# Pooled attention and eight experts on one core: from the fourth expert on, x is gathered as quarter rows and turned on VectorE

## The chip, the cores and the metric

The kernel runs on one core of a Trainium2 chip. The metric is the device time of one execution in microseconds (us). A kernel is timed in several executions; the times below are the median and the spread of three. A profile is one execution, recorded by the hardware profiler, and its span is a little shorter than that execution's time, because the start and the end of the program lie outside it.

The core has five engines, each with an instruction stream that it works through in order: TensorE (PE: matmuls and transposes by matmul; its weight loads are listed as PEld), VectorE (DVE), ScalarE (ACT), GpSimd (POOL) and SyncE (SP, which here only issues DMAs). Engines wait for one another through semaphores. An instruction that waits holds up everything behind it on its own engine.

## The reference

First comes attention with pooled keys and values, then a routing that gives each of 4608 tokens to one of eight experts, 576 tokens to each, and then the experts' two matrix products:

```python
def _moe_ref(x, w_gate, w1, w2):
    N, D = x.shape                      # 4608, 512
    E = w_gate.shape[1]; cap = N // E   # 8, 576
    logits = x @ w_gate
    order = np.argsort(-logits.flatten())
    for idx in order:                   # greedy, in order of the logits
        tok, e = idx // E, idx % E
        if assigned[tok] >= 0 or counts[e] >= cap: continue
        assigned[tok] = e; counts[e] += 1
    for e in range(E):
        mask = assigned == e
        h = np.maximum(x[mask] @ w1[e], 0.0)   # w1: 512 x 1024
        out[mask] = h @ w2[e]                  # w2: 1024 x 512
```

Before it, `x` is softmax(q k_p) v_p over 8 batches and 8 heads of 576 positions, with k and v averaged over groups of eight; the rows of `x` are 512 numbers.

## The kernel before

The first 150 us or so are attention. Its result, the rows of `x`, is written to a buffer `xd` in DRAM, 2 KB a row. After that the kernel works expert by expert, numbered e0 to e7 here in the order in which they are worked off. For each expert:

- **Routing** (class `Routing`). An expert's tokens are found by a threshold search (`search`; some rounds, each of nine matmuls of 128x32 on TensorE, small VectorE steps and two small matmuls, the last of them with `ones`), and `close` turns the marked tokens into a list: `eid` is the number of the expert that was closed, `rows` the 576 row numbers as 128 x 5 numbers, `halves` numbers for half rows. `close` ends in eight matmuls with `spread` (L798) that bring the numbers to their partitions, and in two VectorE steps (L802, L806). Routing of one expert runs beside the matrix products of the expert ahead of it, in pieces.
- **x.** `gather` (L1037) fetches 576 rows from `xd` into `xg` by five indirect DMAs on GpSimd, four of 128 rows and one of 64. `xt` turns one of the five tiles of tokens (a "turn"; tiles 0 to 4): four TensorE transposes into the PSUM tile `tp` (L1069), a ScalarE copy to `xh` that rounds to the fast fp32 format (L1071), and a VectorE subtraction that leaves the rest, `xl` (L1073).
- **Weights.** `load_1` and `load_2` fetch w1 and w2 on SP's queue; ScalarE and VectorE split them likewise into high and low parts (`w1h`, `w1l` at L1049, `w2h`, `w2l` at L1058), eight pieces of 128x512 for each matrix.
- **Stage 1** (`stage1`, L1093). Three products, xh·w1h, xh·w1l and xl·w1h, each in four slices of 128, for eight blocks of 128 rows of h: 96 matmuls for columns 0 to 255 (tiles 0 and 1), then 96 for columns 256 to 575 (tiles 2, 3 and 4). So tiles 0 and 1 must be turned when the expert begins, and the other three when the first half of stage 1 ends. The steps after a block are `hh` on ScalarE (L1098) and `hl` on VectorE (L1101).
- **Stage 2** (`stage2`, L1127, and L1132 for the last 64 tokens). 96 matmuls of 512 columns for four tiles of tokens, 16 pairs for the last; then `put` copies the result (`yt`, `yh`) and GpSimd scatters it to `out` by an indirect DMA (`scatter`, L1107).

What stands where in each engine's stream is decided when the program is built, by a planner in `experts`. It has a clock, `now`, that goes forward with every matmul that it emits, and a clock for VectorE, `dve`. Between two matmuls, `advance` may emit what is due: a routing piece (`step`), a piece of a weight split (`Pieces`), a subtraction that was put off (`later`, `flush`), or a turn (`turns`, `turn`). The clock only chooses the order; on the chip each engine goes as fast as its waits allow. One rule for the turns reads

```python
        t = turned.get(e, 5)
        if t < upto and due(e, "rows", 6.5 + 1.3 * t) and now >= last + 1.4 and (fresh or through or t < late):
            last = now
            turn(e, t)
```

so that a turn often stands right behind a routing matmul (`fresh`), and `gather` is emitted in one piece at the routing step that yields `rows`.

Of the kernel before, what the change touches and what calls it, by code (L numbers as in the profile page):

```python
# [423 lines left out]
class Routing:  # L424
# [56 lines left out]
    def more(self):  # L481
# [10 lines left out]
        nc.vector.tensor_scalar(self.spread[:, 96:128], t, 0.0, None, op0=OP.is_equal)  # L492

        self.blk = cst.tile([128, 20, NC], BF, name="blk")
        nc.scalar.activation(self.blk[:, :18], self.i36[:, 1:19, None].to_broadcast([128, 18, NC]), AF.Copy)
# [219 lines left out]
    def close(self, k, last):  # L715
# [58 lines left out]
        for b0, b1 in halves:  # L774
# [19 lines left out]
            t0, t1 = b0 // 4, b1 // 4  # L794
            ps = self.psum()
            for g in range(4):
                for v in range(2):
                    nc.tensor.matmul(ps[:, :t1 - t0], self.spread[:, 96 - 32 * g:224 - 32 * g], cpv[:, v, :, g],  # L798
                                     start=(g == v == 0), stop=(g == 3 and v == 1))
# [184 lines left out]
class Experts:  # L984
# [27 lines left out]

    def load_1(self, eid, q0=0, q1=4):
# [45 lines left out]

    def xt(self, t, name="tp", bufs=2, later=lambda after, t, f: f()):  # L1060

# [5 lines left out]
        ps = self.psA.tile([128, 4, 128], F32, name=name, bufs=bufs)  # L1067
        for j in range(4):
            nc.tensor.transpose(ps[:, j, :n], self.xg[:n, t, 128 * j:128 * j + 128], self.ident[:n, :n])  # L1069
        o = slice(128 * t, 128 * t + n)  # L1070
        nc.scalar.activation(self.xh[:, :, o], ps[:, :, :n], AF.Copy)  # L1071
        xl, xh = self.xl[:, :, o], self.xh[:, :, o].bitcast(F32)
        later(1.3, 0.65, lambda: nc.vector.tensor_tensor(xl, ps[:, :, :n], xh, op=OP.subtract))  # L1073

# [37 lines left out]

    def stage2(self, e, rows, halves, parts=range(5), bank=("h", 5)):
        for t in parts:
            ps = self.psA.tile([128, 512], F32, name=bank[0], bufs=bank[1])
            yield from self.products(e, t, ps)
            self.put(t, ps, rows, halves)
            yield 0.2275 if t < 4 else 0.44
# [17 lines left out]

    def put(self, t, ps, rows, halves):

        if t < 4:
            y = self.wk.tile([128, 512], F32, name="yt", bufs=2)  # L1140
            self.nc.scalar.activation(y, ps, AF.Copy)  # L1141
            self.scatter(self.out, rows[:, t:t + 1], y)
        else:
            y = self.wk.tile([128, 256], F32, name="yh", bufs=2)
            self.nc.scalar.activation(y, ps[:, :256], AF.Copy)
            self.scatter(self.out.rearrange("n (a d) -> (n a) d", a=2), halves, y)

# [54 lines left out]
def experts(ctx, tc, g, R, xd, w1, w2, out, ident, cap, keep):  # L1202
# [15 lines left out]
    now, dve, ready = 0.0, 0.0, 0.0  # L1218

    def later(after, t, f):  # L1220

        waiting.append((now + after, t, f))
# [8 lines left out]
    def step(e):  # L1231

        nonlocal now, ready, dve, fresh, coming, through
        if held:
# [6 lines left out]
        if what == "id":  # L1241

            if p > e or p and pieces[p - 1].l < 8:
                held.append((p, crit, t, what))
                return False
            X.load_1(R.eid, 0, 4 if p else 2)
            eids[p] = R.eid
        elif what == "rows":
            if p and turned[p - 1] < 5:
                held.append((p, crit, t, what))  # L1250
                return False
            X.gather(R.rows, *R.found)
            if R.found[1] == 5:
# [9 lines left out]
    def advance(e, t, quiet=False):  # L1263

        nonlocal now, fresh
        now += t
        fresh = False
        while True:
            if waiting and waiting[0][0] <= now:
                flush(len(waiting) - 1)  # L1270
            elif ready > now or quiet or first(e) or not step(e):
                break

    def due(e, what, t):
# [45 lines left out]
    def turn(e, t, name="tp", bufs=2):  # L1320

        nonlocal now
# [32 lines left out]
    for i in range(4):  # L1355
        w1.next(i < 3)
    since[0, "rows"] = -7.0

    step(0)
# [9 lines left out]
    for e in range(8):  # L1369
# [5 lines left out]
        for n, dt in enumerate(X.stage1(later, not e)):  # L1375
# [5 lines left out]
            if n == (84 if e else 40):  # L1381
                for t in range(turned[e], 5):
                    turn(e, t)
            if n >= 64 and n % 2:
                w2.by((n - 70) // 14 if n > 70 else 0)
# [13 lines left out]
        w1 = pieces[e + 1] = Pieces(e + 1, X.high1, X.low1)  # L1399
        for n, dt in enumerate(X.stage2(e, *toks[e], range(5 if more else 1))):  # L1400

# [5 lines left out]
        if more:  # L1407
# [5 lines left out]
            for t in range(turned[e + 1], 2):  # L1413
                turn(e + 1, t)
        flush(2)
    flush()
    ps = psB.tile([128, 512], F32, name="h", bufs=5)
# [85 lines left out]
```

## Time and profile before

| | |
|---|---|
| median of three executions | 612.34 us (612.32 to 613.32) |
| the profiled execution | 612.35 us |
| its span | 609.9 us |
| mean granted TensorE clock | 0.984 |
| e0 to e7 | from 157.1 us of the span to its end |

The profiled execution's time is the median's to 0.01 us, and 2.45 us of it lie outside the span. In the lines shown below, a group gives the source line, the engine, the operation, what it writes and reads, the count, and busy time or durations; a row of a timeline gives start and duration in us, where "x4" is four like instructions in a row and the duration is that of the group. Matmuls are pipelined, so that four matmuls that start 0.12 us apart overlap in such a row; what one costs in the stream is the distance from start to start.

### The profile page before, as it was taken

How to read it: one execution, taken by the hardware profiler on the slowest of the kernel's cores; microseconds unless marked ns; L12 is line 12 of the kernel's file. 1: busy time of each engine (PE TensorE's matmuls, PEld its weight loads, DVE VectorE, ACT ScalarE, POOL GpSimd, SP SyncE). 2: the span in 40 equal slices, each digit the busy share in tenths (PEclk: the TensorE clock that was granted, in tenths of full speed). 3: DMA queues.
4: the chain of work that ended last, by engine and by line, in shares of the span. 5: the costliest groups of instructions: out<-in, count | busy, mean ns of one | idle time of the engine just before them, and what ended most of it. 6: DMA issues, size and time to landing. Idle time of an engine off the chain costs nothing.

```text
span 609.9 us, 11520 instructions
## 1 busy us (share of the span) xinstructions
PE 591.5 (97%) x4340; PEld 518.3 (85%) x4340; DVE 396.1 (65%) x1164; ACT 240.0 (39%) x562; POOL 177.3 (29%) x222
## 2 busy tenths in 40 slices
PE   8999999985999999999999999999999999999996
PEld 5999999983797799779977987898799889888975
DVE  7578888987885778767964976487367328503500
ACT  7444444461461434233432452255135325513411
POOL 2999999001200500420312301130221123011012
PEclk9999999995999999999999999999999999999999
DMA  8999972223531740616403701540081037014011
GB/s 353 419 420 423 397 274 82 77 100 98 167 116 31 254 147 22 213 62 219 134 35 116 284 1 52 207 174 18 36 323 57 34 120 278 2 52 166 1 40 43
DMA packets 32641, 92.23 MB, mean 151 GB/s; under 512 B 3488, under 2 KB 3488, under 8 KB 29888
## 3 DMA queue, kind: packets, MB, share of 16 engines
q1 hardware_dynamic: 21296, 62.92, 27.5%
q0 software_dynamic: 5952, 19.01, 9.2%
q10 hardware_dynamic: 5328, 9.48, 4.1%
q8 instruction: 35, 0.57, 0.4%
q14 instruction: 30, 0.25, 0.1%
HBM read 72.53 MB, written 18.87 MB: 150 GB/s over the span
## 4 chain that ended last, share of the span: by engine, by line
PE 81%; issue 7%; DVE 4%; DMA 3%; POOL 3%; ACT 1%; SPq 0%; POOLq 0%; ACTq 0%; another core or an unknown queue 0%; DVEq 0%
PE h L1093 32%; PE h L1127 25%; PE psa L272 6%; PE pss L227 5%; PE h L1132 4%; PE tp L1069 3%; DMA rawk<-in_k_dram 2%; PE pse L256 2%; PE rt L256 1%; PE rt L668 1%; DMA out_dram<-yt,rows 1%; PE rt L630 1%; DMA xg<-xd,rows 1%; PE rt L217 1%; DVE e L238 1%
## 5 line engine op out<-in xcount | busy, mean ns | idle before, releaser
L1127 PE MATMUL h<-w2l,hh 128*128 128x512 f32 x256 | 101.8, 398 | 0.0
L1127 PE MATMUL h<-w2h,hh 128*128 128x512 f32 x256 | 101.4, 396 | 0.3 <-PEq L1193 0.3
L1127 PE MATMUL h<-w2h,hl 128*128 128x512 f32 x256 | 101.5, 396 | 0.0
L1107 POOL DMA_INDIRECT out_dram<-yt,rows x29 | 30.3, 1045 | 232.3 <-ACT yt L1141 231.9
L1098 ACT ACTIVATE hh<-h 128x320 fp32r<-128x320 f32 (+1 forms) x128 | 52.5, 410 | 106.6 <-PE h L1093 103.3
L1093 PE MATMUL h<-xh,w1h 128*128 128x320 f32 (+1 forms) x512 | 93.2, 301 | 0.2 <-ACT xh L1071 0.2
L1093 PE MATMUL h<-xl,w1h 128*128 128x320 f32 (+1 forms) x512 | 93.4, 300 | 0.0
L1101 DVE SCALAR_TENSOR_TENSOR hl<-h,hh 128x320 fp32r<-128x320 f32 (+1 forms) x128 | 57.2, 451 | 53.1 <-ACT hh L1098 34.6
L1093 PE MATMUL h<-xh,w1l 128*128 128x320 f32 (+1 forms) x512 | 91.0, 298 | 0.0
L1093 PEld LDWEIGHTS h<-xh,w1h 128*128 128x128 f32 x512 | 75.7, 190 | 3.4 <-issue 2.7
L1093 PEld LDWEIGHTS h<-xl,w1h 128*128 128x128 f32 x512 | 76.1, 190 | 0.4
L1093 PEld LDWEIGHTS h<-xh,w1l 128*128 128x128 f32 x512 | 75.8, 189 | 0.0
L1037 POOL DMA_INDIRECT xg<-xd,rows x40 | 39.3, 982 | 101.9 <-DVE halves L806 52.7
L1141 ACT ACTIVATE yt<-h 128x512 f32<-128x512 f32 x32 | 19.1, 598 | 112.1 <-PE h L1127 67.4
L272 PE MATMUL psa<-vblk,eT 128*128 128x146 f32 (+3 forms) x390 | 59.9, 302 | 0.2
L1127 PEld LDWEIGHTS h<-w2h,hh 128*128 128x128 f32 x256 | 48.2, 188 | 9.3 <-issue 0.7
L1127 PEld LDWEIGHTS h<-w2l,hh 128*128 128x128 f32 x256 | 48.3, 189 | 8.8
L1127 PEld LDWEIGHTS h<-w2h,hl 128*128 128x128 f32 x256 | 48.2, 188 | 8.8
L272 PEld LDWEIGHTS psa<-vblk,eT 128*128 128x128 f32 (+1 forms) x390 | 50.9, 180 | 1.8 <-issue 0.3
L1049 DVE TENSOR_TENSOR w1l<-raw,w1h 128x512 fp32r<-128x512 f32 x64 | 41.7, 685 | 13.4 <-ACT w1h L1045 13.1
L1073 DVE TENSOR_TENSOR xl<-tp,xh 128x512 fp32r<-128x512 f32 (+1 forms) x40 | 25.3, 633 | 37.4 <-ACT xh L1071 37.3
L1058 DVE TENSOR_TENSOR w2l<-raw,w2h 128x512 fp32r<-128x512 f32 x64 | 43.2, 682 | 2.0 <-ACT w2h L1055 1.8
(224 smaller groups left out, 903.3 us busy)
## 6 DMA issues: line engine op xcount, KB each, us to landing
raw<-in_moe_w_dram SPq DMA_DIRECT2D x64, 512.0 KB, 6.3
xd<-xt ACTq DMA_DIRECT2D x36, 256.0 KB, 5.6
rawv<-in_v_dram SPq DMA_DIRECT2D x7, 1280.0 KB, 14.1
rawk<-in_k_dram SPq DMA_DIRECT2D x7, 1152.0 KB, 11.7
rawq<-in_q_dram SPq DMA_DIRECT2D x7, 1152.0 KB, 11.8
rawk<-in_k_dram SPq DMA_DIRECT2D x2, 576.0 KB, 4.7
rawv<-in_v_dram SPq DMA_DIRECT2D x1, 768.0 KB, 8.0
rawq<-in_q_dram SPq DMA_DIRECT2D x1, 640.0 KB, 9.0
```

The source lines that it names most:

```text
L227: nc.tensor.matmul(ps[cols, j // 2, 144 * (j % 2):144 * (j % 2) + 144], self.q_of(b, j, n, cols.stop - cols.start), self.kblk[b % 4][:, j] ...
L272: self.nc.tensor.matmul(o[h], self.eT[i][:, c, h], self.vblk[b % 4][:, self.BLOCKS[c]:self.BLOCKS[c + 1]], start=(c == cs[0]), stop=(c == ...
L1037: nc.gpsimd.indirect_dma_start(out=self.xg[:n, t, :], out_offset=None, in_=self.xd, in_offset=bass.IndirectOffsetOnAxis(ap=rows[:n, t:t + ...
L1049: self.nc.vector.tensor_tensor(l, raw, h.bitcast(F32), op=OP.subtract)
L1058: self.nc.vector.tensor_tensor(self.w2l[:, i], self.raw2[e][:, i], self.w2h[:, i].bitcast(F32), op=OP.subtract)
L1073: later(1.3, 0.65, lambda: nc.vector.tensor_tensor(xl, ps[:, :, :n], xh, op=OP.subtract))
L1093: nc.tensor.matmul(ps[:, :m], a[:, j, fs], b[:, j, o], start=(n == 0), stop=(n == 11))
L1098: nc.scalar.activation(hh[:, f, o], ps[:, :m], AF.Relu)
L1101: later(0.65, 0.4, lambda f=f, o=o, m=m, ps=ps: nc.vector.scalar_tensor_tensor(hl[:, f, o], ps[:, :m], 0.0, hh[:, f, o].bitcast(F32), op0= ...
L1107: st = nc.gpsimd.indirect_dma_start(out=rows, out_offset=bass.IndirectOffsetOnAxis(ap=idx, axis=0), in_=y, in_offset=None)
L1127: nc.tensor.matmul(ps, a[:, f, o], b[:, f], start=(f == 0 and k == 0), stop=(f == 7 and k == 2))
L1132: nc.tensor.matmul(ps[64 * a:64 * a + 64, :256], self.hr[:, f], self.raw2[e][:, f, 256 * a:256 * a + 256], start=(f == 0), stop=(f == 7))
```

## The change

For the experts e3 to e7:

- `close` multiplies the numbers of the list with a constant `copies` (two matmuls of 128x18 more) and VectorE makes `quarters` from it (one step more): 18 x 128 numbers, one for each quarter row of 128 numbers (512 bytes) of the 576 rows, so that the four quarters of a row come to four different groups of 32 partitions.
- `quarter` replaces `gather`: 18 indirect DMAs of 128 quarter rows for each expert instead of five of rows. They are emitted one at a time (`wanted`, `fetch`), on a clock of GpSimd, `pace`, that counts 1.3 for each indirect DMA, and scatters are put off by 1.0 on the planner's clock and take their place in the same order (`stores`).
- `xt` has VectorE transpose the tile in blocks of 32x32, from `xg` into the PSUM tile `tp` (one instruction of 128 x 512 numbers, or 128 x 256 for tile 4, read with a stride of four numbers), instead of the four TensorE transposes. The ScalarE copy and the subtraction stay.
- The slices of x then hold rows 4p+j of x's transposed form in place of rows 128j+p, and `load_1` fetches w1 in the same arrangement.
- The planner counts 1.1 on VectorE's clock for such a turn instead of 0.45 on TensorE's, waits for `landed` (the time of the DMAs by its own count), and lets a turn of e3 to e7 go where VectorE's clock is not ahead. For all experts the conditions of the turns and of `flush` change.

```diff
+        self.copies = cst.tile([128, 4, 32], F16, name="copies")
...
             ps = self.psum()
+            if k > 2:
+                for v in range(2):
+                    nc.tensor.matmul(ps[:, 16:34], self.copies.rearrange("p a i -> p (a i)"), cp[:, v, :18],
+                                     start=(v == 0), stop=(v == 1))
+                self.quarters = wk.tile([128, 18], I32, name="quarters", bufs=3)
+                nc.vector.tensor_scalar(self.quarters, ps[:, 16:34], self.acol, 0.0, op0=OP.add, op1=OP.max)
...
-        src = self.w1[ds(r, 1)].rearrange("o (j p) f -> p (o j) f", p=128)
+        src = self.w1[ds(r, 1)].rearrange("o (p j) f -> p (o j) f" if quarters else "o (j p) f -> p (o j) f", p=128)
...
+    def quarter(self, idx, n):
+        if not n:
+            self.xg = self.buf("xg", [128, 5, 512])
+        t, g = divmod(n, 4)
+        self.nc.gpsimd.indirect_dma_start(out=self.xg[:, t, 128 * g:128 * g + 128], out_offset=None,
+                                          in_=self.xd.rearrange("n (a d) -> (n a) d", a=4),
+                                          in_offset=bass.IndirectOffsetOnAxis(ap=idx[:, n:n + 1], axis=0))
...
-        for j in range(4):
+        if quarters:
+            nc.vector.transpose(ps[:, :, :n].rearrange("p j (g i) -> p g j i", i=32),
+                                self.xg[:, t, :4 * n].rearrange("p (g i j) -> p g j i", j=4, i=32))
+        for j in range(0 if quarters else 4):
             nc.tensor.transpose(ps[:, j, :n], self.xg[:n, t, 128 * j:128 * j + 128], self.ident[:n, :n])
...
-        later(1.3, 0.65, lambda: nc.vector.tensor_tensor(xl, ps[:, :, :n], xh, op=OP.subtract))
+        later(1.8 if quarters else 1.3, 0.65, lambda: nc.vector.tensor_tensor(xl, ps[:, :, :n], xh, op=OP.subtract))
...
+    def quarters(e):
+        return e > 2
+    def fetch():
+        nonlocal pace
+        e, n, idx = wanted.pop(0)
+        X.quarter(idx, n)
+        pace = max(pace, now) + 1.3
+        if n % 4 == 3 or n == 17:
+            landed[e, n // 4] = pace + 3.7
...
+        if stores and now >= stores[0][0]:
+            stores.pop(0)[1]()
+            pace = max(pace, now) + 1.3
+        elif wanted and now >= pace:
+            fetch()
...
-        now = max(now, since[e, "rows"] + 6.0 + 1.3 * t) + 0.45
+        while (e, t) not in landed:
+            fetch()
+        now = max(now, landed[e, t])
         flush(1)
-        X.xt(t, name, bufs, later_low)
+        if quarters(e):
+            dve = max(dve, now) + 1.1
+        else:
+            now += 0.45
+        X.xt(t, name, bufs, later_low, quarters(e))
...
-        if t < upto and due(e, "rows", 6.5 + 1.3 * t) and now >= last + 1.4 and (fresh or through or t < late):
+        if t < (5 if quarters(e) else upto) and now >= landed.get((e, t), now + 1) + (1.5 if quarters(e) else 0.5) and now >= last + 1.4 and (
+                t < late or (dve <= now if quarters(e) else fresh or through)):
```

The planner's new counts move the routing steps, the turns and the gathers in the streams. The line numbers of the changed kernel differ: matmuls of stage 1 L1093 become L1118, those of stage 2 L1127 become L1152, the turn's L1069 becomes L1091 (VectorE) or L1094 (TensorE, e0 to e2), `xl` L1098, the gathers L1059 and L1049, the scatters L1132. Three places follow.

On TensorE, in the first half of e3's stage 1 (256 columns). Before, the routing of the next expert has closed, its two small matmuls (with `untri` and `tri`) stand there, and the turn of tile 3 stands right behind them:

```order
L1093 MATMUL h<-xh,w1l 128x256 x4
L1093 MATMUL h<-xl,w1h 128x256 x3
L738 LDWEIGHTS untri
L738 MATMUL rt<-ones,untri 128x1
L739 LDWEIGHTS tri
L739 MATMUL rt<-inc,tri 128x1
L1069 MATMUL tp<-ident,xg 128x128 x4
L1093 MATMUL h<-xl,w1h 128x256
```

Now the last small matmul of the search's last round (`ones`, 128x16) stands near the end of that half, 14 matmuls ahead of the first one of the second half (320 columns):

```order
L701 LDWEIGHTS ones
L701 MATMUL rt<-g_254,ones 128x16
L1118 MATMUL h<-xl,w1h 128x256 x2
L1118 MATMUL h<-xh,w1h 128x256 x4
L1118 MATMUL h<-xh,w1l 128x256 x4
L1118 MATMUL h<-xl,w1h 128x256 x4
L1118 MATMUL h<-xh,w1h 128x320 x3
```

The search's end has moved from e2's stage 2 to the end of the first half of e3's stage 1, and no turn stands on TensorE.

On VectorE, at the same end of the search. Before, the steps from `inc` to `eid` are followed by two pieces of w1 and the list's first steps (`si`, `sab`); the turns of tiles 0 to 2 stand ahead of these rows, and those of 3 and 4 behind them:

```order
L729 SCALAR_TENSOR_TENSOR inc<-ones,own 128x36
L731 TENSOR_SCALAR eid<-fm 1x1
L732 TENSOR_SCALAR eid<-eid 1x1
L1049 TENSOR_TENSOR w1l<-raw_3860,w1h 128x512 x2
L1101 SCALAR_TENSOR_TENSOR hl<-h,hh 128x256
L742 SCALAR_TENSOR_TENSOR si<-inc,rt,own 128x36
```

Now the transposes of tiles 3 and 4 stand behind `eid`, with tile 3's subtraction between them:

```order
L736 SCALAR_TENSOR_TENSOR inc<-ones,own 128x36
L738 TENSOR_SCALAR eid<-fm 1x1
L739 TENSOR_SCALAR eid<-eid 1x1
L1091 STREAM_TRANSPOSE tp<-xg 128x4x4x32
L1098 TENSOR_TENSOR xl<-tp,xh 128x4x128
L1091 STREAM_TRANSPOSE tp<-xg 128x2x4x32
L1126 SCALAR_TENSOR_TENSOR hl<-h,hh 128x256
L1080 TENSOR_TENSOR w2l<-raw_4400,w2h 128x512
L1098 TENSOR_TENSOR xl<-tp,xh 128x4x64
L749 SCALAR_TENSOR_TENSOR si<-inc,rt,own 128x36
```

The two last turns of e3 have come behind the search's end on VectorE.

On GpSimd, at e3's list. Before, its five gathers stand between the last scatter of e1 (`yh`) and the first of e2 (`yt`):

```order
L1107 DMA out_dram<-yh,halves 9216x256
L1037 DMA xg<-xd,rows 128x512 x4
L1037 DMA xg<-xd,rows 64x512
L1106 MEMSET spacer 1x1
L1107 DMA out_dram<-yt,rows 4608x512
```

Now twelve of e3's quarter gathers stand among e2's scatters. The last of the twelve is here, behind e2's fourth scatter; the other six of e3 follow e2's last scatter, and then e4's first five, which another list (`quarters_4800`) feeds (the numbers tell the buffers apart):

```order
L1132 DMA out_0_dram<-yt_4357,rows_3392 4608x512
L1049 DMA xg_4165<-xd_62,quarters_4125 128x128
L1131 MEMSET spacer_1808 1x1
L1132 DMA out_0_dram<-yh_4387,halves_3456 9216x256
L1049 DMA xg_4165<-xd_62,quarters_4125 128x128 x6
L1049 DMA xg_4825<-xd_62,quarters_4800 128x128 x5
```

The gathers of one list have come apart, and no longer stand ahead of all scatters of the expert before. The list of e3 now comes 21 matmuls into e2's stage 2 instead of in e2's stage 1; those of e4 to e6 come near the end of the stage 1 of the expert ahead, and e7's, 77 matmuls into it.

More of the change, by code (lines that the diff above doesn't have):

```diff
@@ L492, in more @@
         nc.vector.tensor_scalar(self.spread[:, 96:128], t, 0.0, None, op0=OP.is_equal)
+        self.copies = cst.tile([128, 4, 32], F16, name="copies")
+        nc.vector.tensor_scalar(self.copies, self.spread[:, None, 96:128].to_broadcast([128, 4, 32]), 4.0, None, op0=OP.mult)
+        t = cst.tile([128, 1], I32, name="ta")
+        nc.vector.tensor_scalar(t, self.pq, 5, None, op0=OP.arith_shift_right)
+        self.acol = cst.tile([128, 1], F32, name="acol")
+        nc.vector.tensor_scalar(self.acol, t, -4.0, None, op0=OP.add)
         self.blk = cst.tile([128, 20, NC], BF, name="blk")
@@ L1011, in piece, with load_1 @@
         return slice(i % 4, i % 4 + 1), slice(512 * (i // 4), 512 * (i // 4) + 512)
-    def load_1(self, eid, q0=0, q1=4):
+    def load_1(self, eid, q0=0, q1=4, quarters=False):
         nc = self.nc
@@ L1058, in low2, with xt @@
         self.nc.vector.tensor_tensor(self.w2l[:, i], self.raw2[e][:, i], self.w2h[:, i].bitcast(F32), op=OP.subtract)
-    def xt(self, t, name="tp", bufs=2, later=lambda after, t, f: f()):
+    def xt(self, t, name="tp", bufs=2, later=lambda after, t, f: f(), quarters=False):
         nc = self.nc
@@ L1111, in scatter, with stage2 @@
         self.scatters.append(st)
-    def stage2(self, e, rows, halves, parts=range(5), bank=("h", 5)):
+    def stage2(self, e, rows, halves, parts=range(5), bank=("h", 5), store=lambda f: f()):
         for t in parts:
@@ L1116, in stage2 @@
             yield from self.products(e, t, ps)
-            self.put(t, ps, rows, halves)
+            self.put(t, ps, rows, halves, store)
             yield 0.2275 if t < 4 else 0.44
@@ L1135, in products, with put @@
                     yield 0.44
-    def put(self, t, ps, rows, halves):
+    def put(self, t, ps, rows, halves, store=lambda f: f()):
         if t < 4:
@@ L1141, in put @@
             self.nc.scalar.activation(y, ps, AF.Copy)
-            self.scatter(self.out, rows[:, t:t + 1], y)
+            store(lambda: self.scatter(self.out, rows[:, t:t + 1], y))
         else:
@@ L1145, in put @@
             self.nc.scalar.activation(y, ps[:, :256], AF.Copy)
-            self.scatter(self.out.rearrange("n (a d) -> (n a) d", a=2), halves, y)
+            store(lambda: self.scatter(self.out.rearrange("n (a d) -> (n a) d", a=2), halves, y))
 def wake(nc, wk, w2, numbers):
@@ L1231, in step @@
     def step(e):
-        nonlocal now, ready, dve, fresh, coming, through
+        nonlocal now, ready, dve, fresh, coming, through, pace
         if held:
@@ L1245, in step @@
                 return False
-            X.load_1(R.eid, 0, 4 if p else 2)
+            X.load_1(R.eid, 0, 4 if p else 2, quarters(p))
             eids[p] = R.eid
@@ L1251, in step @@
                 return False
-            X.gather(R.rows, *R.found)
+            if quarters(p):
+                wanted.extend((p, n, R.quarters) for n in range(18))
+                pace = max(pace, now + 1.5)
+            else:
+                X.gather(R.rows, *R.found)
+                for t in range(*R.found):
+                    landed[p, t] = now + 6.0 + 1.3 * t
             if R.found[1] == 5:
@@ L1272, in advance, with store @@
                 break
+    def store(f):
+        stores.append((now + 1.0, f))
     def due(e, what, t):
@@ L1320, in turn @@
     def turn(e, t, name="tp", bufs=2):
-        nonlocal now
-        now = max(now, since[e, "rows"] + 6.0 + 1.3 * t) + 0.45
+        nonlocal now, dve
+        while (e, t) not in landed:
+            fetch()
+        now = max(now, landed[e, t])
         flush(1)
-        X.xt(t, name, bufs, later_low)
+        if quarters(e):
+            dve = max(dve, now) + 1.1
+        else:
+            now += 0.45
+        X.xt(t, name, bufs, later_low, quarters(e))
         turned[e] = t + 1
@@ L1357, in experts @@
     since[0, "rows"] = -7.0
+    landed.update({(0, t): 1.3 * t - 1.0 for t in range(5)})
     step(0)
@@ L1383, in experts @@
                     turn(e, t)
+            if n in ((7, 103) if e else (7, 55)) and lows:
+                flush()
             if n >= 64 and n % 2:
@@ L1399, in experts @@
         w1 = pieces[e + 1] = Pieces(e + 1, X.high1, X.low1)
-        for n, dt in enumerate(X.stage2(e, *toks[e], range(5 if more else 1))):
+        for n, dt in enumerate(X.stage2(e, *toks[e], range(5 if more else 1), store=store if more else lambda f: f())):
             advance(min(e + 1, 7), dt, n >= 96)
@@ L1415, in experts @@
         flush(2)
+        if stores:
+            stores.pop(0)[1]()
     flush()
```

3 lines of the change are left out of this document (2 added, 1 removed).

## The prediction

> **What bounds the kernel now.** I read the page's busy times first, then its chain of waits, then each expert's stretch by itself, and last the timeline around single turns.
>
> ```profile
> span 609.9 us, 11520 instructions
> PE 591.5 (97%) x4340; PEld 518.3 (85%) x4340; DVE 396.1 (65%) x1164; ACT 240.0 (39%) x562; POOL 177.3 (29%) x222
> ...
> PE 81%; issue 7%; DVE 4%; DMA 3%; POOL 3%; ACT 1%; SPq 0%; POOLq 0%; ACTq 0%; another core or an unknown queue 0%; DVEq 0%
> PE h L1093 32%; PE h L1127 25%; PE psa L272 6%; PE pss L227 5%; PE h L1132 4%; PE tp L1069 3%; DMA rawk<-in_k_dram 2%; PE pse L256 2%; PE rt L256 1%; PE rt L668 1%; DMA out_dram<-yt,rows 1%; PE rt L630 1%; DMA xg<-xd,rows 1%; PE rt L217 1%; DVE e L238 1%
> ```
>
> TensorE is busy 97% of the span, and the turn's transposes (`tp`, L1069) are 3% of the chain that ended last. The stretches of e3 to e7, one row each:
>
> ```profile
> core 0: us, PE busy (x) PEld busy (x) DVE busy (x) ACT busy (x) POOL busy (x), PEclk, DMA share, GB/s
> 330.20:386.70 56.50, 56.50 (x406) 48.79 (x404) 36.95 (x115) 21.17 (x50) 10.68 (x15) 1.00 0.33 117
> 386.70:443.30 56.60, 56.60 (x407) 48.88 (x405) 36.92 (x115) 21.14 (x50) 10.68 (x15) 1.00 0.33 117
> 443.30:497.60 54.30, 54.30 (x362) 48.38 (x360) 29.57 (x83) 21.25 (x50) 10.17 (x15) 1.00 0.34 122
> 497.60:552.20 54.60, 54.53 (x362) 48.34 (x360) 24.78 (x58) 21.02 (x50) 10.50 (x15) 1.00 0.34 121
> 552.20:609.90 57.70, 52.85 (x331) 46.60 (x329) 13.46 (x30) 15.78 (x40) 6.26 (x11) 0.98 0.17 62
> ```
>
> From e3 to e6 TensorE is busy for the whole of each stretch at clock 1.00, while VectorE has some 20 us or more free and GpSimd about 44 us. So what leaves TensorE's stream leaves the time, unless TensorE must then wait. I therefore price the matmuls removed, and then look for each place where TensorE will wait.
>
> **Matmuls removed.** 25 turns (five in each of five experts) lose four TensorE transposes each. What a turn costs is the distance from start to start:
>
> ```profile
> 389.59 0.16 PE L739 MATMUL rt<-inc,tri 128*128 128x1 bf16 x1
> 389.62 0.64 PE L1069 MATMUL tp<-ident,xg 128*128 128x128 f32 x4
> 390.01 0.37 PE L1093 MATMUL h<-xl,w1h 128*128 128x256 f32 x1
> ...
> 485.24 0.39 PE L1127 MATMUL h<-w2h,hl 128*128 128x512 f32 x1
> 485.47 0.60 PE L1069 MATMUL tp<-ident,xg 128*128 128x128 f32 x4
> 485.82 0.48 PE L1127 MATMUL h<-w2l,hh 128*128 128x512 f32 x1
> 486.14 0.39 PE L1127 MATMUL h<-w2h,hh 128*128 128x512 f32 x1
> ...
> 486.37 0.40 PE L1127 MATMUL h<-w2h,hl 128*128 128x512 f32 x1
> ```
>
> Behind a routing matmul the four take 0.39 us (389.62 to 390.01), and the long first matmul behind them stays, since a routing matmul alone brings it. Between two of the expert's matmuls they take 0.35 us and the next one starts its successor 0.32 instead of 0.23 us later (485.82 to 486.14, against 486.14 to 486.37): 0.44 us. Of the 25 turns 17 stand behind a routing matmul and 8 alone: 17 x 0.39 + 8 x 0.44 = 10.2 us. The bounds are 25 x 0.39 = 9.8 and 25 x 0.44 = 11.
>
> **Matmuls added.** Two of 128x18 for each of five experts. The nearest row is the eight matmuls that they join:
>
> ```profile
> L798 PE MATMUL rt<-cp,spread x72: 163/167/187, 148.7 to 507.1; 128*128 128x5 f16 x56, 128*128 128x2 f16 x8, 128*128 128x3 f16 x8
> ```
>
> 0.17 us is the duration; as a small matmul in a run costs the stream only its distance (`tri` to `tp` above: 0.03 us), I take 0.04, so 10 x 0.04 = 0.4 us, between 0.3 and 1.7. In e0 to e2 some turns now stand alone instead of behind a routing matmul: about eight of them at up to 0.05, 0.3 us.
>
> **The transpose on VectorE.** No row shows one. It reads and writes 512 numbers a partition, and the nearest rows of that size are the subtractions:
>
> ```profile
> L1073 DVE TENSOR_TENSOR xl<-tp,xh x40: 406/684/693, 155.4 to 554.8; 128x512 fp32r<-128x512 f32 x32, 128x256 fp32r<-128x256 f32 x8
> L1071 ACT ACTIVATE xh<-tp x40: 383/598/602, 154.6 to 554.4; 128x512 fp32r<-128x512 f32 x32, 128x256 fp32r<-128x256 f32 x8
> ```
>
> Lower end 0.69 us (0.41 for the half tile). Upper end: three times that, 2.1, if the stride of four numbers and the blocks cost extra passes. The planner's 1.1 is only the writer's count. I take 0.9 (0.55 for the half tile), nearer to the row, because numbers and traffic are the same, with something on top because a block must be read before it can be written. Per expert that is 4.2 us on an engine with 20 us free; it costs nothing but where TensorE waits for it.
>
> [...]
>
> **Where TensorE will wait.** Three places, all at e3 or where the planner lets turns stand behind the search on VectorE.
>
> ```profile
> 375.62 0.18 PE L694 MATMUL rt<-g,ones 128*128 128x16 bf16 x1
> ...
> 375.85 0.17 DVE L696 TENSOR_REDUCE up<-rt 128x1 f32<-128x8 f32 x1 [0.58 <-PE rt L694]
> ...
> 377.50 0.14 DVE L732 TENSOR_SCALAR eid<-eid 1x1 int32<-1x1 int32 x1
> 377.57 0.67 DVE L1049 TENSOR_TENSOR w1l<-raw,w1h 128x512 fp32r<-128x512 f32 x1
> ...
> 387.28 0.64 PE L1093 MATMUL h<-xh,w1l 128*128 128x256 f32 x4
> 387.75 0.64 PE L1093 MATMUL h<-xl,w1h 128*128 128x256 f32 x4
> ...
> 486.10 0.60 ACT L1071 ACTIVATE xh<-tp 128x512 fp32r<-128x512 f32 x1 [3.65 <-PE tp L1069]
> 486.73 0.69 DVE L1073 TENSOR_TENSOR xl<-tp,xh 128x512 fp32r<-128x512 f32 x1 [8.47 <-ACT xh L1071]
> ```
>
> (1) *Middle of e3's stage 1.* After the search's last `ones` TensorE has 14 matmuls of 256 columns, 0.47/4 = 0.12 us each, so 1.7 to 1.8 us of work, and then needs `xh` of tiles 2 to 4. VectorE first gets the result (0.23, from 375.62 to 375.85), then runs the steps to `eid` (1.72, to 377.57), then tile 3's transpose (0.9); ScalarE copies it (0.63 to the start of `xl`), VectorE subtracts (0.68), transposes tile 4 (0.55), and ScalarE copies that (0.45). The sum is 5.1 to 5.2, less 1.8: a wait of 3.3 us (2.9 with the lower end, 3.6 with 1.1, 5.1 with 2.1). While VectorE is there, the steps of the list of e4 (`si`, `sab`) stand behind tile 4, and TensorE's `untri` matmuls are in the second half, so nobody else waits first.
>
> (2) *Start of e3.* Between the third round's `ones` and stage 1 TensorE has two matmuls of stage 2 and the last 64 tokens:
>
> ```profile
> 382.78 0.39 PE L1127 MATMUL h<-w2l,hh 128*128 128x512 f32 x1
> 383.10 3.67 PE L1132 MATMUL h<-raw,hr 128*64 128x256 f32 x32
> 386.70 0.74 PE L1093 MATMUL h<-xh,w1h 128*128 128x256 f32 x4
> ...
> 367.05 0.16 DVE L696 TENSOR_REDUCE up<-rt 128x1 f32<-128x8 f32 x1
> 368.56 0.21 DVE L656 SCALAR_TENSOR_TENSOR lo<-steps,up,lo 128x1 f32<-128x1 f32 x1
> 368.69 0.69 DVE L1073 TENSOR_TENSOR xl<-tp,xh 128x512 fp32r<-128x512 f32 x1
> ```
>
> That is 3.6 + 2 x 0.23 = 4.1 us. On VectorE stand 0.23, the round's steps (367.05 to 368.69, 1.64), two `w1l` (0.67 each, at L1049), tile 1's transpose 0.9 and its copy 0.63: 4.7. I take a wait of 0.7 (0.4 to 2).
>
> (3) *e3's stage 2*, where the turn of an e4 tile stands between a round's count and the next step: 0.3 (nothing at 0.69, 2.5 at 2.1). At the other turns of e4 to e7 the same sums leave spare time, the least about 0.9 us at e4's tile 4.
>
> **Gathers.** 18 instead of five for an expert:
>
> ```profile
> L1037 POOL DMA_INDIRECT xg<-xd,rows x40: 914/960/1392, 150.3 to 513.2; - x40
> ...
> 340.36 0.98 POOL L1037 DMA_INDIRECT xg<-xd,rows  x1 [8.45 <-DVE halves L806]
> 341.64 0.96 POOL L1037 DMA_INDIRECT xg<-xd,rows  x1 [0.30 <-issue]
> 345.50 0.91 POOL L1037 DMA_INDIRECT xg<-xd,rows  x1 [0.30 <-issue]
> ...
> DMA to landing us min/median/max: 3.0/3.8/6.3
> ```
>
> They stand 1.28 us apart (340.36 to 341.64), and the last, of 64 rows, takes 0.91: the count of rows hardly matters, so I take 1.28 for 128 pieces of 512 B as well. With five scatters, 23 x 1.28 = 29 us of the 54 of an expert. The tightest is e4: from its first gather (at the end of e3's stage 1) to its last turn (62 matmuls into e4) lie a stage 2 of 96 x 0.23 + 3.6 = 25.7 us, 62 x 0.12 = 7.4 us, and by my estimate some 3 us of routing matmuls, so 36 - 29 - 3.8 leaves some 3 us. At e3 the last gather stands six behind e2's last scatter, 9 us into stage 1, and lands at 13 to 15 us, when tile 4 is wanted at about 15. No cost, a thin cover; if the pieces are slower, TensorE stands at e3's second half and at e4's. The w1 load keeps its count and size of pieces (2 KB), SP's order is as before: nothing.
>
> **The sum**, against the profiled execution's 612.35 (its 609.9 us span and 2.45 around it; the median of runs is 612.34): - 10.2 + 0.4 + 0.3 + 3.3 + 0.7 + 0.3 = - 5.2, which gives 607.1 us.
>
> **The rivals.**
>
> *Nearly the whole gain.* VectorE and ScalarE reach the tiles sooner than my chains say: 612.35 - 10.2 + 0.7 = 602.9. For it speaks VectorE's free time, against it that the steps at (1) are in order on one engine and add up from rows. It is the likelier the nearer the transpose is to 0.69, but 2.9 us at (1) stay even then.
>
> *A slow transpose (slower than before).* Were it 2.1 us, the waits become 5.1, about 2 and 2.5 at (1) to (3), 1 at e4's tile 4 and some 2 in the rest, 12.6 in all: 612.35 - 9.5 + 12.6 = 615.5. It decides from about 1.8 us, where the waits eat the 9.5. For it: it has never run in this trace, and reads across four-number strides. Against it: the longest of the subtractions, of the same size and on the same PSUM tile, took 0.693 us.
>
> *Slow gathers.* 23 in a row at 1.6 us instead of 1.28 would be 7 us later at the end of e4's list, with 3 spare, and 2 us later at e3: about 6 us of new waits, no gain (about 613). For it: the longest gather took 1.39 us, so something can hold one up. Against it: the median is 0.96.
>
> **How the numbers follow.** Within 0.2%, 1.2 us, a measurement of this kernel can hardly be told from no change. My forecast (a gain of 3 to 8 us) has 0.62; nearly the whole gain 0.16; slow gathers 0.10, a third of it each side of no change; slow transposes 0.07; something that the order doesn't show 0.05. So faster 0.82, same 0.09, slower 0.09. The range reaches from the whole gain, 602.5, to the forecast with transposes of 1.5 us and gathers somewhat late, 611.5.
>
> **What would show it.** Right: no `tp` rows on TensorE after e2, stretches of e4 to e7 about 2 us shorter each, transposes of 0.7 to 1.1 us, one idle stretch of about 3 us on TensorE that ends with `xh` 11 to 16 us into e3, none elsewhere over 1 us. Wrong: a transpose over 1.5 us, gathers more than 1.4 us apart, or TensorE waiting for `xg` at e4 to e7.

## The result, and the profile after

Measured beside the kernel before: 648.02 us (643.10 to 648.93, four executions) against 612.33 us, a ratio of 1.056 (1.051 to 1.062). The forecast was 607.1 us, range 602.5 to 611.5. It was wrong.

To read this number one has to know that the same instructions took 611.4 us on a second occasion, 639.4 us on a third and 611.3 us on a fourth, with the kernel before at 612 us each time: the loss of 28 to 37 us comes on some occasions only, and without it the change is worth nothing that can be measured (1.000, 0.999 to 1.002, on the second occasion). The three later occasions were on three different chips, and the chip of the first is not on record, so what differs from occasion to occasion may be the chip; "occasion" stands for both below.

The page of the 648.93 us execution, in the lines that answer to those of before:

```profile
span 647.1 us, 11459 instructions
PE 600.1 (93%) x4250; PEld 521.6 (81%) x4250; DVE 422.9 (65%) x1197; ACT 238.8 (37%) x562; POOL 241.5 (37%) x287
PEclk9999999977999999999988899899799999599999
PE 64%; issue 15%; DVE 11%; POOL 4%; ACT 3%; DMA 1%; another core or an unknown queue 1%; POOLq 1%; SPq 0%; ACTq 0%; DVEq 0%
```

TensorE has 90 matmuls fewer and yet more busy time, the granted clock dips, and the chain now has 15% "issue" (7% before, 11% on the 611.4 us occasion) and 1% of a release that the profile can't name. By expert (e2 to e6), the same execution and, below it, one of the 611.4 us occasion:

```profile
core 0 of [0], span 647.1 us
core 0: us, PE busy (x) PEld busy (x) DVE busy (x) ACT busy (x) POOL busy (x), PEclk, DMA share, GB/s
271.60:336.50 64.90, 59.61 (x419) 50.24 (x417) 43.72 (x140) 20.32 (x49) 17.38 (x22) 0.95 0.28 96
336.50:404.40 67.90, 59.09 (x387) 50.62 (x387) 45.02 (x125) 21.19 (x51) 26.91 (x32) 0.95 0.31 101
404.40:470.00 65.60, 59.58 (x399) 50.55 (x397) 43.21 (x125) 21.32 (x51) 25.83 (x31) 0.92 0.31 104
470.00:524.90 54.90, 53.56 (x356) 46.91 (x354) 40.45 (x111) 21.50 (x51) 23.04 (x27) 1.00 0.35 116
524.90:590.30 65.40, 58.11 (x344) 50.16 (x342) 31.06 (x67) 21.42 (x51) 23.66 (x30) 0.90 0.30 105
```

```profile
core 0 of [0], span 608.4 us
271.40:329.80 58.40, 56.94 (x419) 48.50 (x417) 43.71 (x140) 20.31 (x49) 17.58 (x21) 1.00 0.29 103
329.80:390.20 60.40, 56.49 (x386) 48.87 (x386) 44.87 (x125) 21.25 (x51) 26.93 (x33) 0.97 0.35 116
390.20:445.70 55.50, 55.16 (x399) 47.50 (x397) 43.34 (x125) 21.23 (x51) 26.66 (x31) 1.00 0.35 118
445.70:499.00 53.30, 52.95 (x357) 47.02 (x355) 40.50 (x112) 21.64 (x51) 23.39 (x28) 1.00 0.39 129
499.00:551.70 52.70, 52.23 (x345) 46.60 (x343) 30.41 (x66) 21.65 (x51) 23.59 (x28) 1.00 0.38 126
```

The first table is 6.5, 7.5, 10.1, 1.6 and 12.7 us longer, 38.4 us in all, with nearly the same busy times on VectorE, ScalarE and GpSimd. Measured from start to start of its matmuls, TensorE lost 27 us of that in gaps and some 11 us to matmuls at half clock. Both are worked out by setting the two traces, which hold the same 4250 matmuls in the same order, side by side.

**What the gaps look like.** The timeline of the 648.93 us execution at one search round in e2's stage 2:

```profile
317.35 0.39 PE L675 MATMUL rt<-oh,cmp 128*128 128x32 bf16 x9
...
318.36 0.39 PE L1152 MATMUL h<-w2l,hh 128*128 128x512 f32 x1
319.58 0.94 POOL L1049 DMA_INDIRECT xg<-xd,quarters  x1 [0.30 <-issue]
322.11 0.19 DVE L679 TENSOR_TENSOR diagc<-rt,dq 128x32 f32<-128x32 f32 x1 [4.92 <-remote]
322.58 0.19 PE L687 MATMUL rt<-cnt,fold 128*128 128x8 f16 x1 [3.83 <-DVE cnt L683]
```

and in the 611.4 us occasion at the same round:

```profile
317.20 0.39 PE L675 MATMUL rt<-oh,cmp 128*128 128x32 bf16 x9
317.63 0.19 DVE L679 TENSOR_TENSOR diagc<-rt,dq 128x32 f32<-128x32 f32 x1 [0.57 <-PE rt L675]
```

VectorE needs only the nine matmuls. They stand as done by 317.75, their semaphore arrives at 322.09, and VectorE sits idle for 4.9 us; 0.57 us is what this takes otherwise. VectorE's transposes have no part in this gap: the first one of this execution starts at 326.0. The longest piece is in e6's stage 1, where no wait is named at all:

```profile
548.76 0.30 PE L1118 MATMUL h<-xl,w1h 128*128 128x320 f32 x1 [0.59 <-issue]
549.50 0.30 PE L1118 MATMUL h<-xh,w1h 128*128 128x320 f32 x1 [0.44 <-issue]
550.92 0.43 PE L1118 MATMUL h<-xh,w1h 128*128 128x320 f32 x1 [1.11 <-issue]
...
555.24 0.95 POOL L1049 DMA_INDIRECT xg<-xd,quarters  x1 [0.30 <-issue]
```

Matmuls that start 0.15 us apart otherwise start 0.7 or 1.4 us apart, until 2.5 us after the last of 16 gathers in a row (535.8 to 555.2). All long gaps of this kind stand in a run of gathers or just behind one. In the two longest runs, of 10 and 16, the first gap comes some 10 us behind the beginning; in short runs gaps come sooner (one of 2.5 us starts at 451.47, with the first gather of a run of four), and six of the 13 runs of four gathers or more have none.

The trace of this execution also lacks some of the semaphore events (85 of 1,008 increments of VectorE), and so do the three traces of the third occasion; VectorE's are all there in the traces of the kernel before and of the changed kernel at 611 us. They are missing from some 155 us on, just behind the first gathers of rows (150.0) and long ahead of the first quarter gather (310.4) and the first transpose on VectorE (326.0). So the traces of these occasions differ from the others' already where the changed kernel, like the kernel before, gathers rows and transposes on TensorE; time is lost only later (e0 and e1 take as long as on the 611.4 us occasion).

### The profile page after: what moved, and what is told of

It is laid out like the page before. It is cut to its first block, busy times and chain, and to the rows that moved or that the text cites. A ratio compares the mean times of both kernels' runs of the same rounds, so it can differ in the third digit from the quotient of the medians.

```text
span 647.1 us, 11459 instructions
## 1 busy us (share of the span) xinstructions
PE 600.1 (93%) x4250; PEld 521.6 (81%) x4250; DVE 422.9 (65%) x1197; ACT 238.8 (37%) x562; POOL 241.5 (37%) x287
## 4 chain that ended last, share of the span: by engine, by line
PE 64%; issue 15%; DVE 11%; POOL 4%; ACT 3%; DMA 1%; another core or an unknown queue 1%; POOLq 1%; SPq 0%; ACTq 0%; DVEq 0%
PE h L1118 24%; PE h L1152 18%; PE psa L272 6%; PE pss L227 5%; PE h L1157 3%; POOL xg L1049 3%; PE pse L256 2%; DVE tp L1091 1%; POOL out_dram L1132 1%; PE rt L256 1%; PE tp L1094 1%; PE rt L675 1%; ACT xh L1096 1%; DVE e L238 1%
## 5 line engine op out<-in xcount | busy, mean ns | idle before, releaser
L1049 POOL DMA_INDIRECT xg<-xd,quarters x90 | 89.1, 990 | 105.4 <-DVE quarters L808 79.2
L1152 PE MATMUL h<-w2h,hl 128*128 128x512 f32 x256 | 103.1, 403 | 0.8 <-issue 0.8
L1118 PE MATMUL h<-xh,w1h 128*128 128x320 f32 (+1 forms) x512 | 97.3, 308 | 6.4 <-ACT xh L1096 4.3
L1152 PE MATMUL h<-w2h,hh 128*128 128x512 f32 x256 | 102.7, 401 | 0.5 <-PEq L1218 0.3
L1152 PE MATMUL h<-w2l,hh 128*128 128x512 f32 x256 | 103.1, 403 | 0.0
L1132 POOL DMA_INDIRECT out_dram<-yt,rows x29 | 29.8, 1028 | 194.3 <-ACT yt L1166 191.7
L1118 PE MATMUL h<-xh,w1l 128*128 128x320 f32 (+1 forms) x512 | 96.0, 306 | 2.6 <-issue 2.4
L1118 PE MATMUL h<-xl,w1h 128*128 128x320 f32 (+1 forms) x512 | 95.8, 306 | 2.3 <-issue 2.3
L1118 PEld LDWEIGHTS h<-xh,w1h 128*128 128x128 f32 x512 | 78.6, 196 | 12.1 <-issue 6.3
L1118 PEld LDWEIGHTS h<-xh,w1l 128*128 128x128 f32 x512 | 78.7, 195 | 3.7 <-issue 3.7
L1118 PEld LDWEIGHTS h<-xl,w1h 128*128 128x128 f32 x512 | 78.7, 196 | 3.0 <-issue 2.6
L1152 PEld LDWEIGHTS h<-w2l,hh 128*128 128x128 f32 x256 | 49.3, 193 | 12.9 <-issue 3.6
L1152 PEld LDWEIGHTS h<-w2h,hh 128*128 128x128 f32 x256 | 49.4, 193 | 10.5 <-issue 1.3
L1152 PEld LDWEIGHTS h<-w2h,hl 128*128 128x128 f32 x256 | 49.2, 192 | 9.5 <-issue 0.3
L1096 ACT ACTIVATE xh<-tp 128x512 fp32r<-128x512 f32 (+1 forms) x40 | 22.2, 555 | 65.2 <-DVE tp L1091 48.6
```

The lines of the kernel that those rows point to most:

```text
L1049: self.nc.gpsimd.indirect_dma_start(out=self.xg[:, t, 128 * g:128 * g + 128], out_offset=None, in_=self.xd.rearrange("n (a d) -> (n a) d", ...
L1118: nc.tensor.matmul(ps[:, :m], a[:, j, fs], b[:, j, o], start=(n == 0), stop=(n == 11))
L1132: st = nc.gpsimd.indirect_dma_start(out=rows, out_offset=bass.IndirectOffsetOnAxis(ap=idx, axis=0), in_=y, in_offset=None)
L1152: nc.tensor.matmul(ps, a[:, f, o], b[:, f], start=(f == 0 and k == 0), stop=(f == 7 and k == 2))
```

## The experiments

**The change taken apart.** All four beside the kernel before (611.94 us) on one chip.

*plan_only*: only the new planner, without `copies` and `quarters` in `close`.

```diff
-            if k > 2:
+            if k > 8:
...
     def quarters(e):
-        return e > 2
+        return False
```

> The changed planner alone: for all experts five gathers of rows and TensorE transposes as before, no quarter list; only the new conditions, the deferred scatters and the clock of GpSimd remain. Theory G (runs of many gathers on GpSimd hold TensorE up) and theory V (the transposes on VectorE make the routing late) expect about the time before, 611 to 614 us, with TensorE idle under 2 us in e2 to e6. Theory P (the planner's new order of the routing is what makes TensorE wait) expects most of the loss, 625 us or more.

613.75 us, 1.0031 (1.0015 to 1.0047): the new order alone costs 1.8 us. Theory P falls.

*before_plus_gathers*: 13 more gathers behind each list of e3 to e7.

```diff
+        if more and t1 == 5:
+            spare = self.buf("spare", [128, 4, 128])
+            for i in range(13):
+                nc.gpsimd.indirect_dma_start(out=spare[:, i % 4], out_offset=None, in_=self.xd.rearrange("n (a d) -> (n a) d", a=4),
+                    in_offset=bass.IndirectOffsetOnAxis(ap=rows[:, i % 4:i % 4 + 1], axis=0))
...
-            X.gather(R.rows, *R.found)
+            X.gather(R.rows, *R.found, p > 2)
```

> The kernel before, with 13 more gathers of 128 pieces of 512 bytes behind the five of each of e3 to e7, into a buffer that nobody reads; transposes and order of the rest as before. Theory G expects TensorE's intervals to stretch and its signals to come late some 10 us into each run of gathers, and 8 us or more over 612. Theories V and P expect 612 to 614 us.

612.42 us, 1.0008 (0.9996 to 1.0021): runs of 18 gathers, without any effect on this occasion.

*quarters_tensor_turns*: quarter gathers and list, TensorE transposes.

```diff
-            nc.tensor.transpose(ps[:, j, :n], self.xg[:n, t, 128 * j:128 * j + 128], self.ident[:n, :n])
+            nc.tensor.transpose(ps[:, j, :n], self.xg[:n, t, 128 * (j % 2 if short and t == 4 else j):][:, :128], self.ident[:n, :n])
...
-        X.xt(t, name, bufs, later_low, quarters(e))
+        X.xt(t, name, bufs, later_low, False, quarters(e))
```

> The changed kernel with its 18 quarter gathers an expert, its list and its order, but the tiles turned by four TensorE transposes each (so x is not in the right arrangement: the numbers are not the reference's). Theory G expects the long gaps of TensorE in e2 stage 2, e3, e4 and e6 to stay: 645 us or more (the 10 us of transposes come back, the 3.7 us wait at e3 goes). Theory V expects 615 to 622 us. Theory P expects the same as G here.

618.62 us, 1.0108 (1.0079 to 1.0138), 4.9 us over plan_only, without late signals. That is theory V's range, not G's. Five waits at L811 (1.8 us in the line below, 2.5 us counted from start to start) make up half of the 4.9 us; the other half was not traced:

```profile
PE rt L811 <- DVE quarters L808: 1.8, 5, 0.4
```

*rows_vector_turns*: five gathers of rows, VectorE transposes.

```diff
+        if g == 0:
+            self.nc.gpsimd.indirect_dma_start(out=self.xg[:, t, :], out_offset=None, in_=self.xd,
+                                              in_offset=bass.IndirectOffsetOnAxis(ap=idx[:, t:t + 1], axis=0))
...
-                wanted.extend((p, n, R.quarters) for n in range(18))
+                wanted.extend((p, n, R.rows) for n in range(18))
```

> The changed kernel with its order, its list and its transposes on VectorE, but x fetched by five gathers of rows for each of e3 to e7 (so x is not in the right arrangement: the numbers are not the reference's). Theory G expects the loss to go: 603 to 610 us, with the wait of 3.7 us in the middle of e3's stage 1 left. Theories V and P expect 640 us or more.

611.35 us, 0.9991 (0.9980 to 1.0003). Neither G's 603 to 610 nor V's 640. No part alone gave 648 here, so what remained was the two together, or the occasion: the changed kernel itself was not among these runs.

**The changed kernel again**, unaltered, with two variants beside it.

> The changed kernel unaltered, on another occasion beside the two variants below. Since quarter gathers with TensorE turns took 618.6 us and row gathers with VectorE turns 611.4 us, theory I (the two together hold TensorE up: a run of gathers while VectorE transposes what they fetch) expects 640 to 650 us again, with TensorE's signals late. Theory S (the loss is no property of the instructions: the records of that run lost semaphore events from 154 us on, where its instructions are those of the others) expects about 608 to 614 us.

611.38 us (610.23 to 614.02, ten executions), 1.0001 (0.9987 to 1.0015). Theory I falls in its simple form: both together run without late signals. A third and a fourth time:

> The changed kernel unaltered a third time. If its own time is that of the second occasion: 610 to 614 us, no TensorE signal late, no semaphore event missing, and the waits of 3.7 us, 0.8 us and five of 0.5 us at the same places. If the first occasion's disturbance belongs to this program whenever it is loaded anew: 640 us or more, with late signals from about 300 us on.

> The changed kernel a fourth time, as the mark of the occasion beside the three kernels that have a part of it: about 611 us with no TensorE signal late if it is as on the second occasion, 635 to 649 us with late signals if it is as on the first and third.

639.44 us (635.42 to 639.94), 1.043 (1.038 to 1.047), on the third with late signals, and 611.28 us, 0.9993 (0.9979 to 1.0007), on the fourth without. The three kernels with a part of the change were run beside the fourth, and once more on a further occasion:

> The kernel before with 13 more gathers of 512-byte pieces behind each list of e3 to e7 (they go to a buffer nobody reads), on the same occasion. If a long run of gathers is what delays TensorE where the changed kernel is delayed, it takes 8 us or more over 612 with TensorE's intervals at 0.7 us late in each run of 18; if it needs VectorE's transposes as well, 612 to 613 us.

> Quarter gathers and the changed order with TensorE transposes (x not in the right arrangement, so the numbers are not the reference's), on the same occasion. Gathers alone: 640 us or more where the changed kernel is delayed. Gathers together with VectorE's transposes only: 618 us as before.

> Five gathers of rows and VectorE transposes in the changed order (x not in the right arrangement, so the numbers are not the reference's), on the same occasion. If the count of gathers matters: 611 us whatever the changed kernel does. If VectorE's transposes are what delays TensorE: 630 us or more where the changed kernel is delayed.

> The kernel before with 13 more gathers behind each list. On an occasion with late signals: 620 us or more if long runs of gathers alone bring them, 612 to 613 us if not. Without late signals, 612 us.

> Quarter gathers in the changed order with TensorE transposes (the numbers are not the reference's). On an occasion with late signals: 640 us or more if the quarter gathers bring them, 618 us if VectorE's transposes are needed. Without late signals, 618 us.

> Five gathers of rows an expert in the changed order with VectorE transposes (the numbers are not the reference's). On an occasion with late signals: 611 us if the count of gathers brings them, 630 us or more if the transposes do. Without late signals, 611 us.

611.91 and 611.80, 617.85 and 618.37, 611.71 and 611.02 us: as the first time. But no late signals came to any kernel on these occasions, so the runs don't tell which part brings them. That stays open.

**Where the gain went without late signals.** *late_copies*: the two matmuls by `copies` behind the other nine.

```diff
             ps = self.psum()
-            if k > 2:  (copies matmuls, quarters)
             for g in range(4):
                 ... (spread)
             if k:
                 nc.tensor.matmul(ps[:, 8:16], self.ones, pc, start=True, stop=True)
+            if k > 2:  (copies matmuls, quarters)
```

> The changed kernel with the two matmuls by copies moved behind the eight by spread and the one by ones, so that TensorE's next small matmul no longer waits for VectorE's step quarters: the rows show five waits of 0.5 us there. Both theories expect 2 to 3 us less than the changed kernel in the same job, S about 606 to 611 us, I 637 to 648.

608.49 us, 0.9946 (0.9927 to 0.9965): 2.9 us less than the changed kernel beside it. TensorE no longer waits for `quarters`.

*from_fifth*: late_copies, and e3 as before.

```diff
-            if k > 2:
+            if k > 3:
...
-        return e > 2
+        return e > 3
```

> As late_copies, but quarter gathers and VectorE turns only from the fifth expert on (e4 to e7). The wait of 3.6 us in the middle of e3's stage 1 and the 1.3 us of half clock after it should go from e3, 2 us of transposes come back there; if the planner's order makes the same wait at e4, nothing is won. S expects 603 to 610 us, I 630 us or more.

605.86 us (605.74 to 606.04), 0.9903 (0.9886 to 0.9919). The row that was first among TensorE's waits with late_copies, `PE h L1119 <- ACT xh L1097: 4.3, 3, 3.6`, is gone, and no window of e3 or e4 is at half clock. It beats both kernels on this occasion, by 5.9 and 5.5 us.

*contiguous_read*: the transposes read 32 neighbours instead of every fourth number.

```diff
-    self.xg[:, t, :4 * n].rearrange("p (g i j) -> p g j i", j=4, i=32)
+    self.xg[:, t, :4 * n].rearrange("p (g j i) -> p g j i", j=4, i=32)
```

> The changed kernel, but VectorE's transposes read runs of 32 neighbouring numbers instead of every fourth one (w1 stays in rows 4p+j, so the numbers are not the reference's). If the stride makes the transpose take 1.09 us instead of the subtraction's 0.69, it falls to 0.7 and the two waits at e3 shrink by about 0.9 us together: some 610 us. If the transposing itself sets it, 1.09 us and the time of the changed kernel, 611.4 us, stay.

Its time, 637.97 us, is of the third occasion with late signals and says nothing. Its transposes do; theirs and, below, those of the changed kernel on the 611.4 us occasion:

```profile
L1091 DVE STREAM_TRANSPOSE tp<-xg x25: 437/717/727, 325.6 to 572.9; 128x512 f32<-128x512 f32 x20, 128x256 f32<-128x256 f32 x5
```

```profile
L1091 DVE STREAM_TRANSPOSE tp<-xg x25: 628/1086/1147, 321.2 to 540.3; 128x512 f32<-128x512 f32 x20, 128x256 f32<-128x256 f32 x5
```

The stride costs 0.37 us of 1.09. The wait in the middle of e3's stage 1 is 3.2 instead of 3.7 us there.

*blocks_from_fifth*: from_fifth with the contiguous read, and w1 fetched to fit in eight DMAs.

> The version from_fifth (605.9 us) with the contiguous read, and w1 fetched in the order that fits it, in eight DMAs of 256 KB instead of four of 512 KB. If the contiguous read is quicker, the 0.8 us wait at e5 goes: 605 us. If it isn't, 606 us; later than that if the w1 pieces come late because of the doubled count of DMAs.

> The version with late copies, quarter gathers and VectorE turns from the fifth expert on, transposes that read neighbouring numbers and w1 fetched to fit. On an occasion without late signals: 604 to 606 us, under the 605.9 of the same version with the strided read if the 0.37 us per transpose shortens a wait, the same if none stood behind them (the rows of that version show one wait of 0.8 us). With late signals: 635 to 642 us as before.

640.18 us on the third occasion, with late signals, so the late signals need neither e3's turns nor the strided read. 606.06 us (604.52 to 606.96), 0.9902 (0.9882 to 0.9921), on the further occasion: no better than from_fifth, since hardly anything waited for its transposes.

## Why the prediction was wrong, point by point

**The 37 us.** The step that failed is "what leaves TensorE's stream leaves the time, unless TensorE must then wait", together with the search for waits in the order of the instructions alone. No loss of another kind was priced; only a chance of 0.05 stood for "something that the order doesn't show". TensorE lost its time where no instruction stood in its way: its matmuls and its signals came late (4.2 us at 318.36, matmuls 0.7 and 1.4 us apart at 549 to 556) while GpSimd issued gathers. None of the three signs of being wrong came up: the transposes took 1.09 us, the gathers mostly stood 1.25 us apart, and TensorE waited for no `xg` from e3 on. The rival "slow gathers" looked at the engine at which the gaps point, but for another thing: a gather took 0.946 us, as priced, and VectorE waited for the landing of one, 0.6 us.

What is shown: four loads of three kernels that have both quarter gathers and VectorE turns were hit on two occasions, the kernel before never. What is only argued: that the gathers do it, because the gaps stand in and behind runs of them. Whether the gathers alone would be hit on such an occasion wasn't seen. Two more things stay open: whether it is the chip, and whether the recording has a part in it, for every hit execution has its span and clock on record, and the traces that lose time are those that lack events. So why the signals come late is not known.

**The half clock.** The prediction had no term for what a wait does to the clock afterwards. Of the 38 us, some 11 are matmuls at half speed. The windows behind the first gap shown above:

```profile
318.00:320.00 2.00, 0.75 (x4) 0.28 (x2) 0.00 (x0) 0.00 (x0) 1.39 (x3) 1.00 0.13 43
320.00:322.00 2.00, 0.00 (x0) 0.00 (x0) 0.00 (x0) 0.00 (x0) 0.61 (x2) 0.82 0.22 59
322.00:324.00 2.00, 1.42 (x4) 0.86 (x4) 0.81 (x4) 0.00 (x0) 0.00 (x0) 0.50 0.00 0
324.00:326.00 2.00, 2.00 (x6) 1.56 (x6) 1.57 (x7) 0.60 (x1) 0.78 (x1) 0.50 0.00 0
```

The clock falls to 0.50 during the gap and stays there after TensorE has work again; the records have it in pieces of 3.41 us, or 6.83 and 13.65, and the pieces of one trace start whole steps of 3.41 us apart (321.27, 348.57, 358.81). The step ahead of half clock was not idle throughout. Four steps in a row of the 648.93 us execution:

```profile
345.16:348.57 3.41, 1.66 (x14) 1.37 (x13) 1.43 (x4) 0.38 (x1) 0.67 (x1) 1.00 0.16 44
348.57:351.99 3.42, 3.42 (x19) 3.42 (x17) 2.13 (x7) 1.53 (x4) 0.00 (x0) 0.50 0.01 2
351.99:355.40 3.41, 2.04 (x17) 1.80 (x16) 2.71 (x11) 0.14 (x1) 0.00 (x0) 1.00 0.00 0
355.40:358.81 3.41, 1.22 (x9) 1.12 (x10) 2.27 (x5) 2.38 (x7) 0.00 (x0) 1.00 0.75 244
```

TensorE idles for 1.75 us of the first, and the second is at half clock; it idles for 1.37 us of the third, and the fourth is at full clock. In the 20 traces, from e0 on, half clock followed each of the 24 full-clock steps in which TensorE idled for 1.69 us or more, and none in which it idled for 1.57 us or less. So some 1.7 us of idle time in a step were already enough for half clock here, and the price depended on where the gap lay on these steps: the same wait of 3.7 us in e3's stage 1 was followed by one piece (1.4 us lost) in the profile of the 611.4 us occasion and by two (2.3 us) in that of late_copies. The forecast had such a wait, 3.3 us, and no term for this.

**The 4.3 us between forecast and the undisturbed 611.4.** Term by term:

- *Matmuls removed and added*, -10.2 + 0.4 forecast. From plan_only to the changed kernel on the 611.4 us occasion TensorE's time in e3 to e6, gaps and half clock taken off, falls from 223.9 to 214.7 us (224.2 us from 331.8 to 556.0 less 0.3, and 221.9 us from 329.8 to 551.7 less 7.2), and by 0.9 us each in e2 (two turns of e3) and e7: 11.0 us. Forecast were 9.8 us: the mechanism is right, the size 1.2 us too small.
- *The planner's order in e0 to e2 and behind*, +0.3 forecast: 1.8 us by plan_only. The forecast priced only the turns of e0 to e2 that stand alone.
- *Middle of e3's stage 1*, +3.3 forecast. The timeline of the 611.4 us occasion:

```profile
342.02 0.64 PE L1118 MATMUL h<-xl,w1h 128*128 128x256 f32 x4
342.58 0.14 DVE L739 TENSOR_SCALAR eid<-eid 1x1 int32<-1x1 int32 x1
342.76 1.09 DVE L1091 STREAM_TRANSPOSE tp<-xg 128x512 f32<-128x512 f32 x1
343.88 0.60 ACT L1096 ACTIVATE xh<-tp 128x512 fp32r<-128x512 f32 x1 [3.79 <-DVE tp L1091]
344.51 0.69 DVE L1098 TENSOR_TENSOR xl<-tp,xh 128x512 fp32r<-128x512 f32 x1 [0.66 <-ACT xh L1096]
345.12 0.63 DVE L1091 STREAM_TRANSPOSE tp<-xg 128x256 f32<-128x256 f32 x1
345.78 0.38 ACT L1096 ACTIVATE xh<-tp 128x256 fp32r<-128x256 f32 x1 [1.03 <-DVE tp L1091]
346.22 1.17 PE L1118 MATMUL h<-xh,w1h 128*128 128x320 f32 x3 [3.56 <-ACT xh L1096]
```

  The chain is the one that was added up, link for link; the wait is 3.7 us counted from start to start, and 1.4 us of half clock follow, which were not in the sum.
- *Start of e3*, +0.7: 0.8 measured. *e3's stage 2*, +0.3: nothing.
- *The transpose*, 0.9 us taken: 1.09 (0.63 for the half tile). The stride made the difference: from neighbouring numbers the same transpose took 0.72 us (0.45 for the half tile) in contiguous_read, 0.03 over that run's subtractions (0.69). What the forecast put on top of the subtraction's 0.69 was its author's estimate for the blocks, and the runs show 0.03 us of that; the stride's 0.37 us were priced in the upper end of 2.1 alone. Why the stride costs them was not shown.
- *The two added matmuls*, 0.4 us: this is the term that was mis-sized. They cost little, but behind them TensorE's `spread` matmuls write the same PSUM tile that VectorE's step `quarters` reads, and wait for it:

```profile
413.31 0.21 PE L805 MATMUL rt<-cp,copies 128*128 128x18 f16 x2
413.58 0.23 DVE L808 TENSOR_SCALAR quarters<-rt,acol 128x18 int32<-128x18 f32 x1
413.87 0.35 PE L811 MATMUL rt<-cp,spread 128*128 128x5 f16 x8 [0.34 <-DVE quarters L808]
```

  About 0.49 us from start to start beyond their own time, five times: 2.5 us. Late_copies took 2.9 us off.

Together -11.0 + 1.8 + 3.7 + 1.4 + 0.8 + 2.5 = -0.8 us, against -0.4 us measured (611.38 to 611.75). The 611.4 us lie just inside the range of 602.5 to 611.5, but that is luck: of the gain of 3 to 8 us nothing came.

## What to carry to other kernels

Price a wait on TensorE with the half clock that can follow it: in these traces it did from some 1.7 us of idle time in a step of 3.41 us on, and took 1.4 and 2.3 us behind the same wait of 3.7 us. Look at every new instruction that reads a tile which TensorE writes next: two matmuls that start 0.04 us apart brought a wait of 0.5. Turning a tile on another engine paid here where the turn stood off the path: the same turns from the fifth expert on, with the list step moved, gave 1% (605.9 us) where the signals were not late. A kernel should be timed on more than one occasion and more than one chip before an explanation is sought in its instructions: here 36 us of loss came and went.

## What the runs showed of the hardware that was not expected

- TensorE's semaphore arrived more than 4 us after its matmuls (317.75 to 322.09), and its matmuls started 0.7 and 1.4 us apart with no wait named (548.76 to 555.86), both in the 648.93 us execution; losses of this kind came on two occasions, while the kernel before ran as ever on both (612.33 and 611.91 us). The cause is open.
- TensorE's granted clock went in steps of 3.41 us, and in the 20 traces, from e0 on, a step that was idle for half its length was followed by half clock in the next (1.69 us or more in all 24 cases, never with 1.57 us or less).
- A VectorE transpose of 128x512 fp32 numbers into PSUM took 0.72 us from neighbouring numbers and 1.09 us from every fourth one, against 0.69 us for a subtraction of that size.
- 13 more indirect DMAs in a row for each of five experts cost the kernel before nothing that could be measured (1.0008, 0.9996 to 1.0021) on an occasion without late signals.
